# The bias of the exponentials of an attention kernel, computed on ScalarE and not on VectorE

## The chip, the cores and the metric

The kernel runs on one core of one Trainium2 chip, in one launch. The metric is the device time of the whole program in microseconds (us), the median of several runs. The engines are TensorE (matmuls; PE in the rows, with its weight loads as PEld), VectorE (DVE), ScalarE (ACT), GpSimd (POOL) and SyncE (SP), which issues DMAs. Each engine works through its own list of instructions in order and waits on semaphores for the others.

## The reference, cut to what matters

Three layers follow each other on a batch of 8 sequences of 576 positions: an attention with 8 heads of 64 and a mask by blocks of 64; four attention "experts" with a causal mask of which each position takes its best two; and a gated MLP that mixes along the sequence. The softmax is the same in both attentions:

```python
scores = scale * np.matmul(q, k.transpose(0, 1, 3, 2))
scores = np.where(mask, scores, -1000000000.0)
scores = scores - np.max(scores, axis=-1, keepdims=True)
attn = np.exp(scores)
attn = attn / (np.sum(attn, axis=-1, keepdims=True) + 1e-09)
return np.matmul(attn, v).astype(np.float32)
```

What matters here is the exponential of a score less the maximum of its row. The kernel computes exp(es * s + bias) with bias = nes * m + ln 32, where s are the raw products, m the maximum of a row, es a scale (one number, kept in each partition) and nes its negative. The factor 32 keeps the weights in the range of float16 and goes out again in the division by the sum.

## The kernel before, in words

Heads are worked on in pairs, two heads in the two halves of the partitions. Each of the 8 batches has 4 pairs of the first attention and 2 pairs of experts: 48 pairs. The matmuls take each operand as a sum of two float16 parts, so a product is three matmuls (PROD).

A pair is cut into steps. `scores(p, j)` for j = 0 to 3 takes a part of the rows each (PART: chunk 3; chunks 2 and 0; chunk 1; and the last 64 rows of both heads). It is a generator with four pieces: (1) the matmuls of the scores into one of the four PSUM buffers "duo" (L366 to L384); (2) the maxima of the rows, tensor_reduce on VectorE (L387, L389); (3) the bias for all rows of the step in one small instruction of 1, 2 or 4 elements in each partition (L396, on `st`: plane 0 holds the maxima, plane 1 the biases); (4) the exponentials on ScalarE (L399, L404), from PSUM to a buffer `pf`. With the last exponential the step gives its duo back. So there are 48 x 4 = 192 instructions L396, and 16 of the 48 pairs take es and nes from a tile `mt` instead of `es`.

After that, `weights` rounds `pf` to float16 (L329 on ScalarE, L331 on VectorE or L333 on GpSimd) and subtracts for the second part (L423, VectorE or GpSimd). `weights_t` transposes both by DMA into `pT` (L430), `av` multiplies by the values (L441) and divides (L457 to L464). Beside this run the dense steps: evictions of the transposed inputs (L229, L235), the maxima of the inputs (L283), the projections (L793, L816), and the MLP (L872, L951, L967, L987; its output is evicted by L990).

The order of all pieces is a table of numbers (ORDER): every entry runs the next piece of one step, and each engine gets its instructions in that order. A second table (WAYS) says which engine does which copy. The costs given to `add` were used to make the table; when the kernel is built they only count the pieces.

Of the kernel before, what the change touches and what calls it, by code (L numbers as in the profile page):

```python
# [8 lines left out]
F32 = mybir.dt.float32  # L9
# [7 lines left out]
AF = mybir.ActivationFunctionType  # L17
OP = mybir.AluOpType
# [3 lines left out]
P = 128  # L22
# [10 lines left out]
def attn_moe_gmlp_kernel(  # L33
# [17 lines left out]
    V, A, G, T = nc.vector, nc.scalar, nc.gpsimd, nc.tensor  # L51
# [20 lines left out]
    cst = ctx.enter_context(tc.tile_pool(name="cst", bufs=1))  # L72
# [11 lines left out]
    def mine(tag, i=0):  # L84

        return TILES[tag][:, CUR[0].got[tag][i]]
# [3 lines left out]
    def duo():  # L90
        return mine("duo")
# [252 lines left out]

    LN32 = 3.4657359027997265
    PROD = ((0, 0), (0, 1), (1, 0))

    def scores(p, j):

        ps = duo()  # L350
        ph = ps.rearrange("p (h n) -> p h n", h=2)
        if j == 0:
            p.st = sm.tile([P, 2, 9], F32, name="st")
            p.pf = {}
        pf = p.pf[j] = mine("pf")
        st = p.st
        off = {}
        o = 0
        for c in PART[j]:
            off[c] = o  # L360
            w = P * (c + 1)
            ts = slice(P * c, P * c + P)
            for i, (a, bb) in enumerate(PROD):
                for hh in range(2):
                    hs = slice(64 * hh, 64 * hh + 64)
                    T.matmul(ph[:, hh, o:o + w], p.q[hs, a, ts], p.k[hs, bb, 0:w], start=i == 0, stop=False)  # L366
            for hh in range(2):
                hs = slice(64 * hh, 64 * hh + 64)
                if p.moe:
                    T.matmul(ph[:, hh, o + w - 128:o + w - 64], t_row[hs, 0], t_col[hs], start=False, stop=False)  # L370
            for hh in range(2):
                hs = slice(64 * hh, 64 * hh + 64)
                if p.moe:
                    T.matmul(ph[:, hh, o + w - 64:o + w], t_row[hs, 1], t_col[hs], start=False, stop=True)
                else:
                    T.matmul(ph[:, hh, o + w - 64:o + w], m_row[hs], m_col[hs], start=False, stop=True)  # L376
            o += w
        if j == 3:
            for a, n in HALF:
                for i, (l, r) in enumerate(PROD):  # L380
                    T.matmul(ps[:, MID + a:MID + a + n], p.q[:, l, 512:640], p.k[:, r, a:a + n], start=i == 0,
                             stop=i == 2 and not (p.moe and a))
            if p.moe:
                T.matmul(ps[:, MID + 512:MID + S], identb, t_pk, start=False, stop=True)  # L384
        yield
        for c in PART[j]:
            V.reduce_max(st[:, 0, 2 * c:2 * c + 2], ph[:, :, off[c]:off[c] + P * (c + 1)], axis=AX.X)  # L387
        if j == 3:
            V.reduce_max(st[:, 0, 8:9], ps[:, MID:MID + S], axis=AX.X)  # L389
        yield  # L390
        if j == 1:
            m, o = (st[:, z, 0:8].rearrange("p (a c) -> p a c", a=2)[:, :, 0:2] for z in range(2))
        else:
            s = (slice(6, 8), None, slice(2, 4), slice(8, 9))[j]
            m, o = st[:, 0, s], st[:, 1, s]
        V.tensor_scalar(o, m, p.nes, LN32, op0=OP.mult, op1=OP.add)  # L396
        yield
        if j == 3:
            A.activation(pf[:, 448:1024], ps[:, MID:MID + S], AF.Exp, bias=st[:, 1, 8:9], scale=p.es)  # L399
        n = sum(P * (c + 1) for c in PART[j])  # L400
        for c in PART[j]:
            w = P * (c + 1)
            for hh in range(2):
                A.activation(pf[:, n * hh + off[c]:n * hh + off[c] + w], ph[:, hh, off[c]:off[c] + w], AF.Exp,  # L404
                             bias=st[:, 1, 2 * c + hh:2 * c + hh + 1], scale=p.es)
# [4 lines left out]
    def weights(p, j, way):  # L410

        if j == 0:
            p.p16 = {}
        g = GROUP[j]
        if j < 3:
            p.p16[g] = mine("p16")
        s0, n, o0, per = WCOL[j]
        src = p.pf[j][:, s0:s0 + n]
        t = p.p16[g]
        hi, lo = t[:, o0:o0 + n], t[:, per + o0:per + o0 + n]  # L420
        copy16(hi, src, way[0])
        yield
        (V if way[1] == "D" else G).tensor_sub(lo, src, hi)  # L423

    def weights_t(p, g):
        if g == 0:
            p.pT = {}
        t = p.pT[g] = mine("pT")
        n = 16 if g < 2 else 18
        nc.sync.dma_start_transpose(out=t[:, 0:n * P].rearrange("p (n s) -> p n s", s=P), in_=p.p16[g][:, 0:n * P])  # L430
# [49 lines left out]
    def startup():  # L480
# [227 lines left out]
        def s_wm(n):  # L708
# [3 lines left out]
            for c in range(KH):  # L712
                i = 0
                for d in range(KD):
                    for x, y in PROD:
                        T.matmul(ps[:, c], t["woT"][:, x, d, c, :], hl[:, y, d, :], start=i == 0, stop=i == 11)
# [37 lines left out]
    def dense(b, keep):  # L754
# [25 lines left out]
        def proj(n, i):  # L780
# [8 lines left out]
            for a, w in HALF:  # L789
                m = 0  # L790
                for c in range(KD):
                    for l, r in PROD:
                        T.matmul(ps[:, MID + a:MID + a + w], wqk16[:, l, c, 2 * n + i, :], x16[c][:, r, a:a + w],  # L793
# [15 lines left out]
        def vproj(cs):  # L809
            n = len(cs)  # L810
            ps = duo().rearrange("p (c m) -> p c m", c=2)[:, 0:n]
            for i, c in enumerate(cs):
                m = 0
                for d in range(KD):
                    for l, r in PROD:
                        T.matmul(ps[:, i, :260], x16[d][:, l, P * c:P * c + P], wvg16[:, r, d, :], start=m == 0,  # L816
# [45 lines left out]
        def hv(cs):  # L862
# [5 lines left out]
            for i, c in enumerate(cs):  # L868
                m = 0
                for d in range(KH):  # L870
                    for l, r in PROD:
                        T.matmul(ps[:, i], h16[d][:, l, P * c:P * c + P], wf16[:, r, d, FH:], start=m == 0, stop=m == 5)  # L872
# [357 lines left out]
    def pe(*cols, more=0.0):  # L1230
        return ("PE", more + sum(max(n / 2400 + 0.002, 0.029) for n in cols))

    def act(n, ops=1, each=0.13):
        return ("ACT", 0.000833 * n + each * ops)

    def dve(n=8, ops=1, rate=1.04):
        return ("DVE", (rate * n + 80 * ops) / 1000)
# [62 lines left out]
    def copy_sub(n, hi="ADG", more=()):  # L1300

        a = dict(A=act(n), D=dve(n, rate=0.62), G=pool(n, rate=1.1))
        b = dict(D=dve(n, rate=1.35), G=pool(n))
        return {x + y: [a[x], b[y]] + list(more) for x in hi for y in "DG"}


    def pair_steps(key, due, sc_deps, av_deps, wt, moe):

        def p():
            return PD[key]  # L1310
        for j in range(4):
            n = (1024, 1024, 512, 576)[j]
            cols = ((512,) * 3, (384, 128) * 3, (256,) * 3, (288, 288) * 3)[j] + (64,) * (0 if j == 3 and not moe else (1 + (j == 1)) * (1 + moe))
            ops = (1, 2, 1, 1)[j]
            add(("sc", key, j), due + 3 * j, lambda j=j: scores(p(), j),
                [pe(*cols, more=0.2 * (j < 3)), dve(n, ops), dve(), act(n, (2, 4, 2, 1)[j], 0.21)],
                sc_deps, [("sc", key, j - 1)] if j else [], ["duo", "pf"] + [("st", key)] * (j == 0), ["duo"])
        add(("fr", "st", key), due, None, deps=[("sc", key, j) for j in range(4)], rel=[("st", key)])
        add(("fr", "qk", key), due, None, deps=[("sc", key, j) for j in range(4)], rel=[("qk", key)])
        for j in range(4):  # L1320
            n = (1024, 1024, 512, 640)[j]
            add(("w", key, j), due + 3 * j + 4, lambda w, j=j: weights(p(), j, w), copy_sub(n),
                [("sc", key, j), ("su", "abm", 0), ("su", "abm", 1)], [("w", key, 2)] if j == 3 else [], [("p16", (key, j))] if j < 3 else [],
                [("pf", ("sc", key, j))], way=("AG", "DG", "AG", "DD")[j])
        for g in range(3):
            add(("wt", key, g), due + 4 * g + 7, lambda g=g: weights_t(p(), g), [spt((16, 16, 18)[g])],
                [("w", key, j) for j in range(4) if GROUP[j] == g] + [("su", "pad")], [], [("pT", (key, g))], [("p16", (key, g))])
        n = 65
        add(("av", key), due + 18, lambda: av(p(), wt),
            [pe(*[65] * 24), pe(*[65] * 24), pe(*[65] * 42)] + [dve()] * (2 + (wt is not None)) + [dve(640)],  # L1330
            [("wt", key, g) for g in range(3)] + av_deps, [], ["duo", ("x32", key)],
            ["duo"] + [("pT:%d" % g, (key, g)) for g in range(3)])
        add(("x", key), due + 22, lambda w: halves(p(), w), copy_sub(640, more=[spt(10)]),
            [("av", key), ("su", "split", 0), ("su", "split", 1)], [],
            [("xh", key), ("x", key)], [("x32:1", key), ("xh", key)], way="GG")
# [206 lines left out]
```

## Time and profile before

| | us |
|---|---|
| median of 3 runs | 1118.19 |
| lowest and highest | 1117.58 and 1120.28 |
| the profiled execution | 1121.58 |
| its span, first to last instruction | 1119.9 |
| mean granted TensorE clock in it | 0.908 |

The profile is of one execution. Busy times of the engines are sums over their instructions; a stretch is a part of the span; the chain is followed back from the last instruction, at each step to what released it. A wait is the idle time of an engine just before an instruction, put down to the instruction that ended it.

### The profile page before, as it was taken

What the parts mean: (1) busy time and instruction counts of PE and PEld (TensorE: products, weight loads), DVE (VectorE), ACT (ScalarE), POOL (GpSimd) and SP (SyncE); (2) the same over time, 40 slices, a digit from 0 to 9 for tenths busy, and PEclk for the clock granted to TensorE, in tenths of its full rate; (3) what the DMA queues carried; (4) which work ended last, traced back from release to release, by engine and by line L of the source; (5) the groups of instructions that cost most, each with busy time, mean ns of one, the idle gap of its engine ahead of it and who ended that gap; (6) DMA issues with size and microseconds to landing.
All of it is one profiled execution on the core that took longest, in us unless ns stands there. A gap on an engine that the chain in (4) does not pass through costs nothing.

```text
span 1119.9 us, 25239 instructions
## 1 busy us (share of the span) xinstructions
PE 906.4 (81%) x10122; PEld 654.0 (58%) x10122; DVE 885.8 (79%) x1776; ACT 591.0 (53%) x999; POOL 481.7 (43%) x373
## 2 busy tenths in 40 slices
PE   1555568867989888887898887889897999899778
PEld 1344446655666666555675665656774677666444
DVE  2799899899999889888978797968887788657451
ACT  3576566454655555554646455546655564344222
POOL 3636555364254426452544325442775353423110
PEclk9688676878999989998999998999898989999979
DMA  9557969797568948589458974986666456802701
GB/s 197 133 134 146 183 156 154 133 176 158 87 138 161 184 85 144 95 177 166 99 117 157 174 130 93 143 172 116 131 135 142 96 91 116 168 17 39 147 1 43
DMA packets 503028, 143.64 MB, mean 128 GB/s; under 512 B 491200, under 2 KB 497392, under 8 KB 502912
## 3 DMA queue, kind: packets, MB, share of 16 engines
q1 hardware_dynamic: 486176, 134.62, 63.4%
q10 hardware_dynamic: 15296, 3.65, 2.0%
q0 software_dynamic: 1440, 3.78, 1.2%
q8 instruction: 79, 1.29, 0.5%
q14 instruction: 37, 0.30, 0.1%
HBM read 38.19 MB, written 9.44 MB: 43 GB/s over the span
## 4 chain that ended last, share of the span: by engine, by line
PE 25%; DVE 21%; ACT 6%; DMA 5%; issue 4%; POOL 3%; SPq 2%; ACTq 0%; DVEq 0%; POOLq 0%
PE duo L967 5%; PE duo L987 4%; DVE st L387 4%; PE duo L441 3%; PE duo L872 3%; ACT pf L404 3%; DMA pT<-p 3%; PE duo L793 2%; DVE p L331 2%; PE duo L366 2%; DVE p L423 2%; PE duo L816 2%; PE duo L951 1%; DVE st L396 1%; DVE vn L916 1%
## 5 line engine op out<-in xcount | busy, mean ns | idle before, releaser
L423 POOL TENSOR_TENSOR p<-pf,p 128x1024 f16<-128x1024 f32 (+2 forms) x121 | 228.4, 1892 | 210.8 <-ACT p L329 93.8
L404 ACT ACTIVATE pf<-duo,st,es 128x128 f32<-128x128 f32 (+3 forms) x256 | 139.0, 620 | 106.6 <-DVE st L396 77.3
L441 PEld LDWEIGHTS <-pT 128*128 128x128 f16 x4320 | 153.1, 101 | 38.5 <-DMA pT<-p 16.8
L387 DVE TENSOR_REDUCE st<-duo 128x2 f32<-128x1024 f32 (+1 forms) x192 | 151.0, 815 | 14.8 <-PE duo L376 7.5
L967 PE MATMUL duo<-wsp,vn 128*128 128x288 f16 x896 | 127.9, 299 | 18.0 <-DVE x L464 6.5
L366 PE MATMUL duo<-qk 64*128 64x256 f16 (+3 forms) x1152 | 112.3, 312 | 36.3 <-DVE qk L806 11.9
L987 PE MATMUL duo<-wo,gT 128*128 128x512 f16 (+1 forms) x480 | 114.1, 395 | 8.9 <-ACT pf L404 7.3
L793 PE MATMUL duo<-x,wqk 128*128 128x288 f16 x768 | 106.3, 302 | 16.6 <-ACT pf L399 13.9
L441 PE MATMUL duo<-v,pT 128*128 128x65 f16 (+1 forms) x2880 | 108.3, 199 | 13.7 <-DMA pT<-p 7.5
L967 PEld LDWEIGHTS <-vn 128*128 128x128 f16 x896 | 90.1, 102 | 46.4 <-issue 12.8
L404 ACT ACTIVATE pf<-duo,st,mt 128x512 f32<-128x512 f32 (+3 forms) x128 | 69.8, 619 | 72.0 <-DVE st L396 58.6
L793 PEld LDWEIGHTS <-wqk 128*128 128x128 f16 x768 | 78.4, 103 | 42.0 <-issue 18.2
L333 POOL TENSOR_SCALAR p<-pf 128x1024 f16<-128x1024 f32 (+2 forms) x41 | 43.9, 1071 | 126.0 <-ACT pf L404 76.1
L423 DVE TENSOR_TENSOR p<-pf,p 128x640 f16<-128x640 f32 (+2 forms) x71 | 83.5, 1178 | 10.2 <-ACT p L329 4.9
L987 PEld LDWEIGHTS <-gT 128*128 128x128 f16 (+1 forms) x480 | 48.5, 104 | 66.0 <-issue 15.7
L331 DVE CAST p<-pf 128x512 f16<-128x512 f32 (+2 forms) x82 | 64.5, 791 | 28.1 <-ACT pf L404 12.8
L366 PEld LDWEIGHTS <-qk 64*128 64x128 f16 x1152 | 47.8, 97 | 66.1 <-issue 51.4
L283 DVE TENSOR_REDUCE mst<-nat 128x1 f32<-128x640 f32 (+1 forms) x56 | 61.2, 1095 | 26.8 <-DMA nat<-in_k_dram 16.5
L910 POOL TENSOR_SCALAR vf<-vf,nw 128x512 f32<-128x512 f32 (+1 forms) x35 | 33.3, 958 | 80.5 <-DVE nw L901 62.5
L322 PE MATMUL duo<-ident,nat 128*128 128x128 f32 (+1 forms) x320 | 53.2, 302 | 14.6 <-ACT pf L404 5.4
L441 PE MATMUL duo<-V,pT 128*128 128x65 f16 (+1 forms) x1440 | 53.9, 198 | 12.8 <-DMA pT<-p 8.0
L816 PE MATMUL duo<-wvg,x 128*128 128x260 f16 x480 | 60.9, 287 | 3.7 <-ACT pf L404 2.6
(250 smaller groups left out, 1737.4 us busy)
## 6 DMA issues: line engine op xcount, KB each, us to landing
out_dram<-o SPq DMA_DIRECT2D x16, 512.0 KB, 3.9
nat<-in_q_dram SPq DMA_DIRECT2D x58, 128.0 KB, 3.3
nat<-in_k_dram SPq DMA_DIRECT2D x58, 128.0 KB, 3.2
nat<-in_v_dram SPq DMA_DIRECT2D x50, 128.0 KB, 3.0
wf<-in_moe_w_in_dram SPq DMA_DIRECT2D x8, 512.0 KB, 5.8
pT<-p SPq DMA_TRANSPOSE x144, 4.8
wf<-in_moe_w_out_dram SPq DMA_DIRECT2D x4, 512.0 KB, 4.4
pT<-in_moe_w_spatial_dram POOLq DMA_DIRECT2D x1, 1152.0 KB, 7.5
```

The costliest lines, as they stand in the source:

```text
L283: V.tensor_reduce(s.st[:, a, pr:pr + 1], t[:, a].rearrange("p i c d -> p i (c d)"), op=OP.max, axis=AX.X, apply_absolute_value=True)
L322: T.transpose(ps[:, P * c:P * c + r], p.nat[0:r, i, c, :], ident[0:r, 0:r])
L331: V.tensor_copy(hi, src)
L366: T.matmul(ph[:, hh, o:o + w], p.q[hs, a, ts], p.k[hs, bb, 0:w], start=i == 0, stop=False)
L387: V.reduce_max(st[:, 0, 2 * c:2 * c + 2], ph[:, :, off[c]:off[c] + P * (c + 1)], axis=AX.X)
L404: A.activation(pf[:, n * hh + off[c]:n * hh + off[c] + w], ph[:, hh, off[c]:off[c] + w], AF.Exp, bias=st[:, 1, 2 * c + hh:2 * c + hh + 1], ...
L423: (V if way[1] == "D" else G).tensor_sub(lo, src, hi)
L441: T.matmul(ps[:, hh, o:o + n], pT[:, col(t, kk):col(t, kk) + P], p.v[:, hh, kk, a:a + n], start=kk == 0 and i == 0, stop=kk == nk - 1 and ...
L793: T.matmul(ps[:, MID + a:MID + a + w], wqk16[:, l, c, 2 * n + i, :], x16[c][:, r, a:a + w], start=m == 0, stop=m == 11)
L816: T.matmul(ps[:, i, :260], x16[d][:, l, P * c:P * c + P], wvg16[:, r, d, :], start=m == 0, stop=m == 11)
L967: T.matmul(ps[:, MID + a:MID + a + n], vn[:, l, ds_], wsp16[:, r, c, a:a + n], start=i == 0, stop=False)
L987: T.matmul(ps[0:r, i], gT[:, x, d, P * c:P * c + r], wo16[:, y, d, :], start=m == 0, stop=m == 11)
```

## The change

A tile of one column, `ln32`, is filled with ln 32 once. The small instruction of piece (3) is no longer a tensor_scalar of VectorE (times nes, plus a constant) but an activation of ScalarE with the function Identity, scale nes and bias `ln32`. The table of the order and the ways stay as they are. In the call of `add` the third piece has ScalarE's cost in place of VectorE's.

```diff
     LN32 = 3.4657359027997265
     PROD = ((0, 0), (0, 1), (1, 0))
+    ln32 = cst.tile([P, 1], F32, name="ln32")
+    V.memset(ln32, LN32)
...
-        V.tensor_scalar(o, m, p.nes, LN32, op0=OP.mult, op1=OP.add)
+        A.activation(o, m, AF.Identity, bias=ln32, scale=p.nes)
         yield
...
-                [pe(*cols, more=0.2 * (j < 3)), dve(n, ops), dve(), act(n, (2, 4, 2, 1)[j], 0.21)],
+                [pe(*cols, more=0.2 * (j < 3)), dve(n, ops), act(8), act(n, (2, 4, 2, 1)[j], 0.21)],
```

The lines of the kernel move down by two, so that L396 becomes L398, L399 and L404 become L401 and L406, and L423 becomes L425.

The first place is the one at 620 to 628 us of the trace. On VectorE before, L396 stands three times, each a few instructions behind its reduction; the third (128x1) belongs to the reduction L389 and stands behind a cast:

```order
L396 TENSOR_SCALAR st<-st,es 128x2x2
L387 TENSOR_REDUCE st<-duo 128x2
L235 SCALAR_TENSOR_TENSOR v<-nat,scb,v 128x10x64
L396 TENSOR_SCALAR st<-st,es 128x2
L283 TENSOR_REDUCE mst<-nat 128x1
L389 TENSOR_REDUCE st<-duo 128x1
L331 CAST p_140<-pf 128x512
L396 TENSOR_SCALAR st<-st,es 128x1
L423 TENSOR_TENSOR p_140<-pf,p_140 128x512
```

And VectorE at the same place now:

```order
L389 TENSOR_REDUCE st<-duo 128x2
L235 SCALAR_TENSOR_TENSOR v<-nat,scb,v 128x10x64
L283 TENSOR_REDUCE mst<-nat 128x1
L391 TENSOR_REDUCE st<-duo 128x1
L331 CAST p_140<-pf 128x512
L425 TENSOR_TENSOR p_140<-pf,p_140 128x512
```

The three are gone and the others keep their order. On ScalarE at that place before (the maxima are those of the rows above, `o` is the output of the MLP):

```order
L404 ACTIVATE pf<-duo,st,es 128x384 x2
L404 ACTIVATE pf<-duo,st,es 128x128 x2
L404 ACTIVATE pf<-duo,st,es 128x256 x2
L990 ACTIVATE o<-duo,hs 128x1024
L399 ACTIVATE pf<-duo,st,es 128x576
```

ScalarE now:

```order
L398 ACTIVATE st<-st,ln_182,es 128x2x2
L406 ACTIVATE pf<-duo,st,es 128x384 x2
L406 ACTIVATE pf<-duo,st,es 128x128 x2
L398 ACTIVATE st<-st,ln_182,es 128x2
L406 ACTIVATE pf<-duo,st,es 128x256 x2
L992 ACTIVATE o<-duo,hs 128x1024
L398 ACTIVATE st<-st,ln_182,es 128x1
L401 ACTIVATE pf<-duo,st,es 128x576
```

Each bias stands right in front of the exponentials that use it. The second place is at 476 us, on ScalarE, where an expert's first bias and the evictions of transposed inputs (`qk`, for the next pair) are near each other. Before:

```order
L990 ACTIVATE o<-duo,hs 128x1024
L229 ACTIVATE qk<-duo,scb 128x640
L229 ACTIVATE qk<-duo,scb 128x576
L404 ACTIVATE pf<-duo,st,mt 128x512 x2
L229 ACTIVATE qk<-duo,scb 128x640
```

Now:

```order
L992 ACTIVATE o<-duo,hs 128x1024
L398 ACTIVATE st<-st,ln_182,mt 128x2
L229 ACTIVATE qk<-duo,scb 128x640
L229 ACTIVATE qk<-duo,scb 128x576
L406 ACTIVATE pf<-duo,st,mt 128x512 x2
L229 ACTIVATE qk<-duo,scb 128x640
```

Here the bias stands in front of two evictions that do not need it.

## Rows read from the trace of the kernel before

**Rows 1.** The page: busy us of each engine (share of the span), instructions

```profile
PE 906.4 (81%) x10122; PEld 654.0 (58%) x10122; DVE 885.8 (79%) x1776; ACT 591.0 (53%) x999; POOL 481.7 (43%) x373
```

**Rows 2.** Stretches: start:end, length, busy us of PE, PEld, DVE, ACT, POOL; clock; DMA

```profile
70.00:400.00 330.00, 248.59 (x2988) 188.24 (x2987) 301.24 (x553) 191.58 (x330) 156.86 (x109) 0.84 0.79 152
400.00:1060.00 660.00, 582.83 (x6734) 418.78 (x6732) 523.26 (x1071) 351.49 (x597) 289.74 (x210) 0.95 0.66 123
```

**Rows 3.** The page: the chain that ended last, by engine and by line

```profile
PE 25%; DVE 21%; ACT 6%; DMA 5%; issue 4%; POOL 3%; SPq 2%; ACTq 0%; DVEq 0%; POOLq 0%
PE duo L967 5%; PE duo L987 4%; DVE st L387 4%; PE duo L441 3%; PE duo L872 3%; ACT pf L404 3%; DMA pT<-p 3%; PE duo L793 2%; DVE p L331 2%; PE duo L366 2%; DVE p L423 2%; PE duo L816 2%; PE duo L951 1%; DVE st L396 1%; DVE vn L916 1%
```

**Rows 4.** Waits: who for whom, us in total, times, longest

```profile
ACT pf L404 <- DVE st L396: 135.9, 66, 5.7
ACT pf L399 <- DVE st L396: 51.4, 23, 6.8
...
PE duo L793 <- ACT pf L399: 13.9, 5, 4.9
...
PE duo L381 <- ACT pf L404: 0.4, 1, 0.4
```

**Rows 5.** Groups of VectorE, L396: busy us, mean ns | idle before

```profile
L396 DVE TENSOR_SCALAR st<-st,es 128x2 f32<-128x2 f32 (+2 forms) x128 | 44.3, 357 | 0.5
L396 DVE TENSOR_SCALAR st<-st,mt 128x2 f32<-128x2 f32 (+1 forms) x64 | 26.6, 421 | 0.5
```

**Rows 6.** Line L396, its larger half: shortest, median, longest in ns

```profile
L396 DVE TENSOR_SCALAR st<-st,es x128: 166/220/2102, 68.4 to 946.2; 128x2 f32<-128x2 f32 x64, 128x4 f32<-128x4 f32 x32, 128x1 f32<-128x1 f32 x32
```

**Rows 7.** Timeline of VectorE and ScalarE, 622 to 628: start, us, engine, line

```profile
622.44 0.75 DVE L389 TENSOR_REDUCE st<-duo 128x1 f32<-128x576 f32 x1
626.79 0.43 DVE L331 CAST p<-pf 128x512 f16<-128x512 f32 x1 [3.61 <-DMA pT<-p]
627.13 0.21 DVE L396 TENSOR_SCALAR st<-st,es 128x1 f32<-128x1 f32 x1
627.26 0.69 DVE L423 TENSOR_TENSOR p<-pf,p 128x512 f16<-128x512 f32 x1
...
623.10 1.14 ACT L990 ACTIVATE o<-duo,hs 128x1024 f32<-128x1024 f32 x1
627.46 0.83 ACT L399 ACTIVATE pf<-duo,st,es 128x576 f32<-128x576 f32 x1 [3.23 <-DVE st L396]
```

**Rows 8.** Timeline of VectorE and GpSimd at 488 us

```profile
488.08 2.13 POOL L423 TENSOR_TENSOR p<-pf,p 128x1024 f16<-128x1024 f32 x1
488.48 1.76 DVE L396 TENSOR_SCALAR st<-st,mt 128x2 f32<-128x2 f32 x1
490.15 0.74 DVE L389 TENSOR_REDUCE st<-duo 128x1 f32<-128x576 f32 x1
```

**Rows 9.** Groups of ScalarE by shape: exponentials of 512 and 128 columns

```profile
L404 ACT ACTIVATE pf<-duo,st,es 128x512 f32<-128x512 f32 x64 | 46.4, 777 | 47.7 <-DVE st L396 27.2 <-DVE hm L927 6.6 <-DVE rr L459 5.6
L404 ACT ACTIVATE pf<-duo,st,es 128x128 f32<-128x128 f32 x64 | 25.9, 464 | 0.0
```

**Rows 10.** Timeline of ScalarE: two exponentials in a row

```profile
68.74 1.45 ACT L404 ACTIVATE pf<-duo,st,es 128x512 f32<-128x512 f32 x2 [1.31 <-DVE st L396]
```

**Rows 11.** Pieces of the chain that ended last: start, us, what

```profile
383.86 0.23 DVE st L396
...
1042.83 0.23 DVE st L396
```

**Rows 12.** The stretch 70 to 400, instructions of L396 alone

```profile
70.00:400.00 330.00, 28.69 (x71) 0.84 0.79 152
```

**Rows 13.** Timeline of VectorE and ScalarE at 476 us

```profile
476.59 1.21 DVE L387 TENSOR_REDUCE st<-duo 128x2 f32<-128x1024 f32 x1
...
477.20 1.43 ACT L229 ACTIVATE qk<-duo,scb 128x640 f16<-128x640 f32 x2 [1.84 <-PE duo L322]
```

**Rows 14.** Groups of ScalarE: the table load

```profile
L586 ACT ACT_TABLE_LOAD x1 | 1.3, 1283 | 18.8 <-DMA nat<-in_v_dram 18.8
```

## The prediction

> **What bounds the kernel now.** I read the busy shares first. TensorE is busy 81% of the span and VectorE 79%, ScalarE only 53% and GpSimd 43% [rows 1]. An average hides two stages, so the stretches come next [rows 2]. From 70 to 400 us VectorE is busy 301.2 of 330 us (91%) and TensorE 248.6 (75%): VectorE is the bound there. From 400 to 1060 us TensorE has 582.8 of 660 (88%), VectorE 523.3 (79%): TensorE leads, and what it waits for counts. The last 60 us are dense work without an exponential. Third is the chain that ended last [rows 3]: TensorE 25% and VectorE 21% of the span, ScalarE 6%. Its shares add up to 66% and its first piece is at 378 us, so it says nothing of the first third. On it the bias (L396) has 1% under its own name. Last the waits [rows 4]: ScalarE sat idle in front of exponentials until a bias of VectorE for 135.9 + 51.4 = 187.3 us, in 89 waits. TensorE in turn waits for exponentials to give a PSUM buffer free: 13 rows, 39 waits, 58.3 us, the first and last of them shown.
>
> The reader is to see a loop: scores, reduction, bias, exponential, buffer free, next matmul. ScalarE is the one engine in it with room.
>
> **What is removed.** 192 small instructions leave VectorE, 44.3 + 26.6 = 70.9 us busy [rows 5]. That is 0.37 us each while the median is 0.220 and the longest 2.1 [rows 6]: a few are long because they stand still. Short ones hold the engine less than they last: at 627.13 one lasts 0.21 and the next instruction starts at 627.26, 0.13 later [rows 7]. So about 192 x 0.13 = 25 us is the pitch, and 70.9 - 192 x 0.21 = 31 us is standing still, 56 us together. One of the long ones shows the cause: it starts at 488.48 and lasts 1.76, ending at 490.24; a subtraction of GpSimd runs from 488.08 to 490.21, and the reduction queued behind starts at 490.15 [rows 8].
>
> The Trainium skill (SBUF — State Buffer, "Who interferes with whom") says that VectorE and GpSimd share one pair of ports as a lock, that a tensor_scalar in a two-port mode may take it and a tensor_reduce never does; by that rule a stall in front of a reduction vanishes with the bias and one in front of a cast may only move to the cast. The ends at 490.24 and 490.21 agree with the lock; that it moves no run here shows yet.
>
> **What is added.** 192 activations on ScalarE, of 1 to 4 elements, with a bias and a scale from memory. The trace has no such size; the exponentials have the same two operands. They last 777 ns at 512 columns and 464 at 128 [rows 9], 0.815 ns a column, so 464 - 126 x 0.815 = 361 ns at 2 columns. Two that follow each other take 1.45 us where 2 x 0.777 were 1.55 [rows 10]: 0.10 overlap, a pitch of 0.26. The dependent exponential may overlap too or not: 0.26 to 0.40; I take 0.31. On ScalarE this is 192 x 0.36 = 69 us more busy time, 591 to 660, 59% of the span. The overlap of 0.10 is seen between instructions without such a dependence, which is why I stay in the middle.
>
> **What moves.** TensorE, GpSimd and the DMA queues keep their instructions and order; no DMA is moved past anything. The one new constant is a memset of VectorE at the start. What changes is where the bias waits. Before, it queued on VectorE behind whatever lay between the reduction and it. At 622.44 a reduction starts and ends at 623.19. Behind it a cast waits for a buffer until 626.79, the bias comes at 627.13, and the exponential at 627.46, although ScalarE had been free since 624.24 [rows 7]. Now the bias stands on ScalarE behind the output eviction: 624.24 + 0.31 = 624.6, 2.9 us earlier. Only a part is worth anything, since that cast still ends at 627.22 and VectorE goes on from there. The opposite case is at 383.86: there the bias was the very next thing after its reduction, 0.23 on the chain [rows 11], and 0.36 replaces it: 0.1 lost. The added wait is that ScalarE now stops at the bias for the reduction. Mostly the exponential is next and would have waited anyway; in 32 of 192 places, by the new order, something else is next.
>
> **The sum.** (a) 70 to 400 us: 71 of the biases, 28.7 us busy [rows 12]. Pitch 71 x 0.13 = 9, stalls 28.7 - 71 x 0.21 = 14: 23 us of a VectorE that is 91% busy. The ends are 0 (the stalls move on and other engines fill the rest) and 23; I take half, 11, since 9% of idle time already shows other limits.
> (b) From 378 us the chain has 49 pieces of L396, 15.1 us in all, the first at 383.86, the last at 1042.83 [rows 11]. 30 of them hand on to VectorE itself, 6.3 us, and simply go. 19 hand on to an exponential, 8.8 us; each becomes 0.31, so 5.9 comes back and 2.9 is the least gain. Where other VectorE work stood between reduction and bias, as at 627, more goes: up to 15 if every such exponential moved its whole way. I take 7. Against it, where ScalarE itself is on the chain without waiting for a bias, a dozen new activations at 0.26 add 3. That is 6.3 + 7 - 3 = 10, of which some is lost when another chain ends last: 8, between -3 and 18.
> (c) From 1060 us: nothing.
> Together 19 us. The profiled execution took 1121.6 us (span 1119.9 and 1.7 around it), 3.4 above the median of the runs, 1118.2; so 1121.6 - 19 = 1102.6 in its terms, and 1099 for the median.
>
> **The rivals.**
> *The stall moves on.* Of (a) only the pitch is left, 9, half of it 5, and (b) loses the long pieces, as the 1.76 at 488.48: about 4. Sum 9: 1109. For it: half the chain goes on with VectorE work, casts among it. Against it: at 488 and 623 the next instruction or the waiting exponential does not need GpSimd. [...]
> *It is hidden anyway.* TensorE has 88% from 400 us on, and the exponentials come earlier into a VectorE queue whose order was laid out for the later time; at 627 the work behind is held by a transpose DMA. Then the gain is under 0.3% (3.4 us, about what a measurement can tell): 1117. Against it: 58.3 us of TensorE's waits are for exponentials.
> *ScalarE's queue stops: slower.* In the 32 places a bias now stands in front of work that was free to run. At 476.59 a reduction starts and ends at 477.80; two evictions of transposes went at 477.20 [rows 13]. With the bias ahead of them they start at 477.80 + 0.36, 1.0 us later, and with them their PSUM buffer. If 20 of the 32 cost 1 us on the path, (a) and (b) are eaten up; if all do, 32 - 19 = 13 slower, and with the 103 biases (192 - 89) whose exponential did not wait a part of 103 x 0.26 = 27 comes on top. I price it at +8: 1126. Against it: ScalarE is busy only 53%.
> The skill's ScalarE: Activation LUTs ("Rules for kernel authors") sends add and multiply to VectorE, not ScalarE, which speaks against this change. By the rows it is 0.36 against 0.21 each; if length alone decided, 49 pieces on the chain would make 49 x 0.15 = 7 us, 1125, which shares this rival's chance. At 627 it is not length that decides but the queue in front of the bias.
> *It does not do what it says:* exponentials with another function between them could reload ScalarE's table. The one load of the trace takes 1.28 us [rows 14]; 192 pairs would give 490 us. The kernel already mixes exponentials, Relu and absolute values with that one load, and the new order has one too. No chance given.
>
> **How the numbers follow.** Forecast (1099, its own range 1090 to 1108) 0.52; the stall moves on (1109) 0.25; hidden (1117) 0.13; slower (1126) 0.10. The first two are faster by over 0.3%: 0.77. Same: 0.13, slower: 0.10. The range takes (a) and (b) near their upper ends, 1118 - 36 = 1082, with under 0.1 left below, and reaches into the hidden case, 1119; what is left above is the slower one.
>
> **What would show it.** L396 gone from VectorE, its busy time down by some 60 to 70 us, its idle time up by less. ScalarE up by 60 to 70 us, the new activations near 0.36 us, still one table load. ScalarE's waits in front of exponentials, 187 us, now in front of the bias and for the reduction, and well under that. TensorE's 58 us of waits for exponentials shorter. Stretches: most gain from 70 to 400 us. If VectorE's casts and subtractions grow by some 20 us together, the stall moved. If evictions (L229 before) wait behind biases and TensorE's waits for them grow, the slower rival is right. The forecast is wrong if VectorE's time falls as said and the span does not.

## The result, and the profile after

The changed kernel takes 1107.63 us (median of 4 runs, 1105.66 to 1110.61), beside 1119.24 for the kernel before on the same chip: 0.9900 of its time [0.9872, 0.9927], some 11 us faster where 19 were forecast. The profiled execution took 1110.61 us (span 1108.9). Like the one of before it is about 3 us above its median, so the two compare evenly.

Busy us of each engine after, to hold against [rows 1]:

```profile
PE 898.7 (81%) x10122; PEld 647.5 (58%) x10122; DVE 846.5 (76%) x1585; ACT 656.4 (59%) x1191; POOL 483.1 (44%) x373
```

VectorE has 191 instructions fewer (192 less the memset) and 39.3 us less busy time, ScalarE 192 more and 65.4 us more. The two stretches after, in the columns of [rows 2]:

```profile
70.00:400.00 330.00, 246.28 (x3024) 184.77 (x3024) 288.22 (x488) 218.61 (x408) 158.84 (x109) 0.88 0.79 152
400.00:1060.00 660.00, 584.67 (x6742) 418.18 (x6741) 502.66 (x958) 393.46 (x715) 289.23 (x210) 0.95 0.67 123
```

In the first, VectorE fell from 301.2 to 288.2, 13 us, and is still busy 87%. The new instruction after (shortest, median, longest in ns; compare [rows 6]):

```profile
L398 ACT ACTIVATE st<-st,ln,es x128: 370/388/407, 69.5 to 944.2; 128x2 f32<-128x2 f32 x64, 128x4 f32<-128x4 f32 x32, 128x1 f32<-128x1 f32 x32
```

It lasts 0.388 us and never stands still. And the waits after (compare [rows 4]): ScalarE's in front of the bias, then the first and the last row of TensorE's for exponentials:

```profile
ACT st L398 <- DVE st L389: 104.2, 71, 5.9
ACT st L398 <- DVE st L391: 50.7, 24, 7.1
...
PE duo L795 <- ACT pf L401: 13.4, 3, 5.4
...
PE duo L953 <- ACT pf L406: 0.8, 1, 0.8
```

ScalarE waits 154.9 us in 95 waits where it was 187.3 in 89. TensorE waits for exponentials in 14 rows, 37 waits, 59.5 us together, against 58.3 before. One of the 37 is the same wait under another name. Before:

```profile
240.46 0.37 PE L197 MATMUL duo<-ident,m 128*3 128x128 f32 x1 [6.74 <-DVE m L290]
```

And after:

```profile
238.96 0.37 PE L197 MATMUL duo<-ident,m 128*3 128x128 f32 x1 [9.61 <-ACT pf L406]
```

TensorE stood idle in front of this matmul in both, before put down to VectorE and after to an exponential. Without it, TensorE's waits for exponentials are 49.9 us, 8 less than before. Kernels that gained nothing or little have sums below 58.3 too (e1, further down, 55.1; e8 52.0), so one profile each does not show whether the gain came through that door.

Where VectorE's room went shows in its groups: busy us, mean ns, then idle us in front of the group and what ended it. Before:

```profile
L423 DVE TENSOR_TENSOR p<-pf,p 128x640 f16<-128x640 f32 (+2 forms) x71 | 83.5, 1178 | 10.2 <-ACT p L329 4.9 <-POOL p L333 4.4 <-issue 0.4
L331 DVE CAST p<-pf 128x512 f16<-128x512 f32 (+2 forms) x82 | 64.5, 791 | 28.1 <-ACT pf L404 12.8 <-DMA pT<-p 5.7 <-ACT pf L399 4.4
L283 DVE TENSOR_REDUCE mst<-nat 128x1 f32<-128x640 f32 (+1 forms) x56 | 61.2, 1095 | 26.8 <-DMA nat<-in_k_dram 16.5 <-DMA nat<-in_v_dram 7.3 <-DMA nat<-in_q_dram 2.2
...
L916 DVE TENSOR_TENSOR vn<-vf,vn 64x512 f16<-64x512 f32 x7 | 15.6, 2229 | 6.1 <-ACT vn L913 6.0
```

And after:

```profile
L425 DVE TENSOR_TENSOR p<-pf,p 128x640 f16<-128x640 f32 (+2 forms) x71 | 77.5, 1093 | 8.4 <-ACT p L329 5.0 <-POOL p L333 2.7
L331 DVE CAST p<-pf 128x512 f16<-128x512 f32 (+2 forms) x82 | 65.8, 807 | 36.8 <-ACT pf L406 12.9 <-ACT pf L401 9.4 <-DMA pT<-p 5.9
L283 DVE TENSOR_REDUCE mst<-nat 128x1 f32<-128x640 f32 (+1 forms) x56 | 61.3, 1097 | 35.3 <-DMA nat<-in_k_dram 21.1 <-DMA nat<-in_v_dram 10.0 <-DMA nat<-in_q_dram 4.0
...
L918 DVE TENSOR_TENSOR vn<-vf,vn 64x512 f16<-64x512 f32 x7 | 20.2, 2893 | 6.5 <-ACT vn L915 6.4
```

VectorE stands 8.5 us more in front of the input maxima, waiting for loads, and 8.7 more in front of the casts. The casts and the subtractions of weights did not grow (148.0 to 143.3 us together). Seven subtractions of 64 partitions in the MLP's normalization (`vn`, L916, now L918) did, from 15.6 to 20.2.

Next, how the lead of after over before runs along TensorE: the same instruction in both timelines (start, us, what). Before:

```profile
398.23 5.36 PE L816 MATMUL duo<-wvg,x 128*128 128x260 f16 x24 [1.67 <-ACT pf L404]
...
785.76 6.05 PE L793 MATMUL duo<-x,wqk 128*128 128x288 f16 x48
...
796.95 1.52 PE L366 MATMUL duo<-qk 64*128 64x512 f16 x5 [2.95 <-DVE qk L806]
...
1061.86 5.31 PE L872 MATMUL duo<-wf,x 128*128 128x512 f16 x16 [2.89 <-DMA x<-xh]
```

After:

```profile
395.30 2.83 PE L818 MATMUL duo<-wvg,x 128*128 128x260 f16 x24 [1.81 <-ACT pf L406]
...
780.44 6.05 PE L795 MATMUL duo<-x,wqk 128*128 128x288 f16 x48
...
796.95 1.53 PE L368 MATMUL duo<-qk 64*128 64x512 f16 x5 [8.25 <-DVE qk L808]
...
1052.63 6.00 PE L874 MATMUL duo<-wf,x 128*128 128x512 f16 x27 [2.02 <-DMA x<-xh]
```

The lead is 2.9 us at 398, 5.3 at 786, nothing at 797, 9.2 at 1062 and 11.0 at the end. Between 786 and 797 all of it is gone: TensorE waits 8.25 us for one VectorE instruction, where before it waited 2.95. VectorE and GpSimd at that place, after:

```profile
787.93 8.18 DVE L918 TENSOR_TENSOR vn<-vf,vn 64x512 f16<-64x512 f32 x1 [1.34 <-ACT vn L915]
796.14 2.09 DVE L808 SCALAR_TENSOR_TENSOR qk<-duo,mt,qk 128x512 f16<-128x512 f32 x4
...
787.95 1.15 POOL L918 TENSOR_TENSOR vn<-vf,vn 128x512 f16<-128x512 f32 x1
789.06 1.14 POOL L425 TENSOR_TENSOR p<-pf,p 128x512 f16<-128x512 f32 x1
790.16 1.55 POOL L266 DMA_DIRECT2D nat<-in_v_dram  x2
791.70 0.61 POOL L269 DMA_DIRECT2D nat<-in_v_dram  x1
792.32 1.16 POOL L918 TENSOR_TENSOR vn<-vf,vn 128x512 f16<-128x512 f32 x1
793.43 2.12 POOL L425 TENSOR_TENSOR p<-pf,p 128x1024 f16<-128x1024 f32 x1
```

The same instruction before:

```profile
793.59 2.53 DVE L916 TENSOR_TENSOR vn<-vf,vn 64x512 f16<-64x512 f32 x1 [0.89 <-ACT vn L913]
...
793.31 1.15 POOL L916 TENSOR_TENSOR vn<-vf,vn 128x512 f16<-128x512 f32 x1
794.42 1.15 POOL L423 TENSOR_TENSOR p<-pf,p 128x512 f16<-128x512 f32 x1
795.52 1.56 POOL L266 DMA_DIRECT2D nat<-in_v_dram  x2
```

The shortest of its line takes 0.68 us. Before, it stood until GpSimd turned to issuing DMAs, and ended at 796.12. After, it arrived 5.7 us earlier, did not get in when GpSimd turned to the same DMAs at 790.16, stood through two more subtractions, and ended at 796.11. What all the rest had gained by then was waited away there. The seven have a second long one, at 677 us before (4.80 us) and at 671 after (4.81); it is in both, so it does not part them.

### The profile page after: what moved, and what is told of

Read it like the earlier page. It is cut to its first block, busy times and chain, and to the rows that moved or that the text cites. A ratio compares the mean times of both kernels' runs of the same rounds, so it can differ in the third digit from the quotient of the medians.

```text
span 1108.9 us, 25219 instructions
## 1 busy us (share of the span) xinstructions
PE 898.7 (81%) x10122; PEld 647.5 (58%) x10122; DVE 846.5 (76%) x1585; ACT 656.4 (59%) x1191; POOL 483.1 (44%) x373
## 5 line engine op out<-in xcount | busy, mean ns | idle before, releaser
L425 POOL TENSOR_TENSOR p<-pf,p 128x1024 f16<-128x1024 f32 (+2 forms) x121 | 229.8, 1904 | 209.2 <-ACT p L329 81.3
L443 PEld LDWEIGHTS <-pT 128*128 128x128 f16 x4320 | 151.5, 101 | 39.2 <-DMA pT<-p 17.1
L389 DVE TENSOR_REDUCE st<-duo 128x2 f32<-128x1024 f32 (+1 forms) x192 | 150.3, 814 | 19.4 <-PE duo L378 9.3
L406 ACT ACTIVATE pf<-duo,st,es 128x128 f32<-128x128 f32 (+3 forms) x256 | 139.5, 616 | 3.6 <-ACT st L398 0.4
L443 PE MATMUL duo<-v,pT 128*128 128x65 f16 (+1 forms) x2880 | 107.5, 198 | 16.8 <-DMA pT<-p 8.8
L398 ACT ACTIVATE st<-st,ln,es 128x2 f32<-128x2 f32 (+2 forms) x128 | 48.3, 387 | 95.8 <-DVE st L389 57.1
L331 DVE CAST p<-pf 128x512 f16<-128x512 f32 (+2 forms) x82 | 65.8, 807 | 36.8 <-ACT pf L406 12.9
L425 DVE TENSOR_TENSOR p<-pf,p 128x640 f16<-128x640 f32 (+2 forms) x71 | 77.5, 1093 | 8.4 <-ACT p L329 5.0
L406 ACT ACTIVATE pf<-duo,st,mt 128x512 f32<-128x512 f32 (+3 forms) x128 | 70.2, 616 | 7.9 <-issue 6.3
L476 POOL TENSOR_TENSOR xh<-x,xh 128x640 f16<-128x640 f32 x30 | 45.8, 1528 | 40.6 <-DVE xh L331 37.2
```

Source lines behind the costliest of these rows:

```text
L331: V.tensor_copy(hi, src)
L398: A.activation(o, m, AF.Identity, bias=ln32, scale=p.nes)
L443: T.matmul(ps[:, hh, o:o + n], pT[:, col(t, kk):col(t, kk) + P], p.v[:, hh, kk, a:a + n], start=kk == 0 and i == 0, stop=kk == nk - 1 and ...
```

## The experiments

Two theories stood at first. A, the load: the gain is VectorE's time, pitch and standing still. B, the place: the gain is that the bias no longer queues behind VectorE's other work. After the first four runs came S, the stall: the one subtraction above takes back part of whatever is gained, so kernels must be compared with it out of the way. "Before" and "changed" are the two kernels of the case; each ratio is against before on the same chip. Differences between ratios carry both intervals, added as squares.

**e1_both.** The changed kernel, with the old instruction left on VectorE, its output read by nobody.

```diff
+        V.tensor_scalar(u, m, p.nes, LN32, op0=OP.mult, op1=OP.add)
         A.activation(o, m, AF.Identity, bias=ln32, scale=p.nes)
```

> The bias on ScalarE as in the changed kernel, and the old instruction also left on VectorE at its old place, writing to a plane that nothing reads. Theory A (the gain is VectorE's room: pitch and standing still of 192 instructions): the gain goes, ratio to the kernel before 0.997 to 1.002. Theory B (the gain is that the bias no longer queues on VectorE behind other work, so exponentials start earlier): the gain stays, 0.988 to 0.993. In between, both in their shares.

Measured: 1.0047 [1.0023, 1.0071], 1122.8 us. All of the gain is gone and a little more (above theory A's range), although the bias stands where the change puts it. So the place alone is not the gain; putting VectorE's instruction back costs 0.0147 ± 0.0037.

**e2_dve_next.** Before, with the bias still on VectorE but directly behind its reduction.

```diff
             V.reduce_max(st[:, 0, 8:9], ps[:, MID:MID + S], axis=AX.X)
-        yield
         if j == 1:
...
         yield
+        yield
         if j == 3:
```

> The bias stays on VectorE, but is issued in the same piece as its reduction, right behind it, so that nothing queues in between. Theory A: VectorE holds the same 192 instructions, no gain, 0.997 to 1.002. Theory B: most of the gain without ScalarE, 0.988 to 0.993.

Measured: 1.0115 [1.0086, 1.0143], 1128.58 us: the earliest place for the bias is the slowest kernel of all, outside the ranges of both theories. Its groups:

```profile
L395 DVE TENSOR_SCALAR st<-st,es 128x2 f32<-128x2 f32 (+2 forms) x128 | 52.7, 411 | 4.5
L395 DVE TENSOR_SCALAR st<-st,mt 128x2 f32<-128x2 f32 x64 | 28.6, 447 | 2.3
```

One place of its timeline:

```profile
76.18 0.75 DVE L389 TENSOR_REDUCE st<-duo 128x1 f32<-128x576 f32 x1
76.96 0.21 DVE L395 TENSOR_SCALAR st<-st,es 128x1 f32<-128x1 f32 x1
```

The bias now takes 81.3 us (70.9 before), and behind its own reduction it starts 0.03 us after that ended, while elsewhere neighbours overlap by 0.08 or 0.09 [rows 7]. VectorE's busy time rose by 21.2 us to 907.0. This speaks for the load and against the place. That it explains the whole 0.0115 is not shown; this profile has the long stall too (8.59 us).

**e3_act_last.** Changed, with the bias moved into the last piece, so that no other ScalarE work stands between it and its exponentials (the slower rival's 32 places are gone).

```diff
-        A.activation(o, m, AF.Identity, bias=ln32, scale=p.nes)
         yield
+        A.activation(o, m, AF.Identity, bias=ln32, scale=p.nes)
         if j == 3:
```

> The changed kernel with the bias issued in the last piece, right in front of its exponentials, so that in none of the 32 places other work of ScalarE stands behind a bias that waits. If those stops cost (the slower rival of the prediction, in part): 0.984 to 0.988. If they cost nothing: as the changed kernel, 0.989 to 0.991. Theories A and B do not differ here.

Measured: 0.9859 [0.9833, 0.9884], 1101.12 us, 0.0041 ± 0.0038 better than changed. But in its profile the subtraction near 788 us takes 2.41 us and not 8.18, so this is not yet the queue's price; e7 asks again.

**e5_act_twice.** Changed, with the bias computed twice on ScalarE.

```diff
+        A.activation(u, m, AF.Identity, bias=ln32, scale=p.nes)
         A.activation(o, m, AF.Identity, bias=ln32, scale=p.nes)
```

> The changed kernel with every bias computed twice on ScalarE, the first into a plane that nothing reads: 192 more activations, some 55 us more of ScalarE's time and 0.29 us later exponentials. If ScalarE has room (both theories as I stated them): 0.990 to 0.994. If the length of the bias on ScalarE counts on the path, 49 pieces of 0.29: 14 us, 1.002.

Measured: 0.9960 [0.9937, 0.9983], 1112.01 us. 192 more activations cost 0.0060 ± 0.0036, and here too the long stall is absent (1.18 us). With the stall only in one of the two, the difference is not a clean price; f4 gives that.

**e6_vn_gpsimd.** Changed, with the 64-partition subtractions always on GpSimd (the second letter of each pair; seven instructions change engine).

```diff
-        "norm.4": ("GG", "DD", "GD", "GD"), ...
+        "norm.4": ("GG", "DG", "GG", "GG"), ...
```

> The changed kernel with one more edit: the last subtraction of the normalised gate (vn, 64 rows, once in each batch) always on GpSimd. In the profile of the changed kernel one of these stood still for 8.2 us on VectorE at 788 us and the lead over the kernel before, 5.3 us, was gone behind it; it did so too with the bias on both engines (8.2) and behind its reduction (8.6), and not with the bias in the last piece or twice. Theory S (that one stall hides half of the change's gain): 0.983 to 0.987, as the version with the bias in the last piece. Theory Q (that version was better because ScalarE's queue no longer stops at a bias): 0.989 to 0.992, as the changed kernel.

Measured: 0.9841 [0.9801, 0.9880], 1100.21 us, 0.0059 ± 0.0048 better than changed. The line in changed and in this kernel:

```profile
L918 DVE TENSOR_TENSOR vn<-vf,vn x11: 676/1220/8184, 309.2 to 1069.7; 64x512 f16<-64x512 f32 x7, 128x512 f16<-128x512 f32 x4
```

```profile
L918 DVE TENSOR_TENSOR vn<-vf,vn x4: 693/1056/1635, 306.6 to 1060.6; 128x512 f16<-128x512 f32 x4
```

And TensorE's waits for `qk` in this kernel:

```profile
PE duo L368 <- DVE qk L808: 7.5, 6, 2.2
```

TensorE's longest wait for `qk` of VectorE is 2.2 us; in changed it was 8.3, as in e1, e2, e8 and e9; before it was 2.9. VectorE is busy 833.6 us, 12.9 less than in changed.

**e7_last_vn_gpsimd.** e3 with the edit of e6.

```diff
-        A.activation(o, m, AF.Identity, bias=ln32, scale=p.nes)
         yield
+        A.activation(o, m, AF.Identity, bias=ln32, scale=p.nes)
...
+        "norm.4": ("GG", "DG", "GG", "GG"), ...
```

> The bias in the last piece, right in front of its exponentials, and vn on GpSimd as in the run before this one. Theory S: no better than vn on GpSimd alone, 0.983 to 0.987. Theory Q: both gains add or the vn edit does nothing, 0.980 to 0.986 and at least 0.004 below vn on GpSimd alone.

Measured: 0.9815 [0.9779, 0.9851], 1096.74 us: the fastest kernel of the study. That is below theory S's range, but not the 0.004 below e6 that theory Q asked for: against e6 it is 0.0026 ± 0.0053 better, which is unclear. So the queue stops of the slower rival cost between nothing and some 9 us; that they cost anything is not shown.

**e8_odd_form.** Before, with the bias on VectorE in a form that does not stand still: the maxima read three times over, 6 or 12 elements, into a tile of its own.

```diff
+                src = m.unsqueeze(1).to_broadcast([P, 3, 2])
+            V.tensor_scalar(ob[:, 0:6 * k].rearrange("p (x y) -> p x y", x=3) if j != 1 else
...
-        V.tensor_scalar(o, m, p.nes, LN32, op0=OP.mult, op1=OP.add)
```

> The kernel before, the bias still on VectorE at its old place, but read three times over (6 or 12 elements out, a source of three rows) into a tile of its own, so that the instruction does not stand still for GpSimd, as its one-element form never did. Theory L (the standing still, 31 of 56 us, is what the change saves): 0.992 to 0.996. Theory P (the pitch of 192 instructions counts as well, or alone): 0.997 to 1.001. If these instructions still last over 0.3 us, the form did not do its work and the run tells nothing.

Measured: 0.9971 [0.9948, 0.9994], 1115.8 us. The form does what it should:

```profile
L404 DVE TENSOR_SCALAR ob<-st,es x96: 158/213/226, 71.4 to 941.4; 128x6 f32<-128x6 f32 x64, 128x12 f32<-128x12 f32 x32
```

Longest 226 ns where it was 2102 [rows 6]. VectorE's busy time fell by 17.1 us, the time by 3 (with the 8.2 us stall in this profile too). The 192 instructions themselves fell from 70.9 to 40.2 us, so the 31 us of standing still that I had counted did go. The engine got 17 of them back; the rest came up again in other instructions, 6.7 us of it in the `vn` subtractions (19.1 to 25.9 us).

**e9_both_odd.** e1, with VectorE's extra instruction in the form of e8.

```diff
+            V.tensor_scalar(ob[:, 0:6 * k].rearrange("p (x y) -> p x y", x=3) if j != 1 else
...
+            V.tensor_scalar(u, m, p.nes, LN32, op0=OP.mult, op1=OP.add)
         A.activation(o, m, AF.Identity, bias=ln32, scale=p.nes)
```

> The bias on ScalarE and the old instruction left on VectorE as well, but in the form of the run before, which does not stand still; its result is read by nothing. Theory L: most of the gain stays, 0.990 to 0.996 (the run with the form that stands still gave 1.0047). Theory P: the gain goes, 0.999 to 1.005.

Measured: 0.9995 [0.9969, 1.0022], 1118.22 us, 0.0052 ± 0.0036 better than e1: the standing still. The rest to changed, 0.0095 ± 0.0038, is the pitch, if the stall (8.20 us here too) weighs the same in both.

**f1 to f4.** Before, e1, e9 and e5, each with the edit of e6, so that the stall is in none of them. The diff is the same in all four.

```diff
-        "norm.4": ("GG", "DD", "GD", "GD"), ...
+        "norm.4": ("GG", "DG", "GG", "GG"), ...
```

> The kernel before with vn on GpSimd, as control: all four runs of this call have that edit, so that the one long stall at 788 us can't be in some and not in others. With the bias on ScalarE this edit gave 0.9841. Theory S (the edit only takes away a stall that the kernel before hardly had): 0.995 to 1.000. If the edit is good by itself: 0.990.

Measured: 0.9993 [0.9970, 1.0017], 1117.47 us: without the change the edit is worth nothing.

> The bias on both engines, the old form on VectorE, vn on GpSimd. The difference to 0.9841 is the price of the 192 instructions on VectorE, pitch and standing still. Theory A: 0.996 to 1.001, so 12 to 17 thousandths. Theory B (their room is worth nothing): 0.984.

Measured: 0.9956 [0.9931, 0.9980], 1114.5 us, 0.0037 ± 0.0034 better than f1: the bias on ScalarE alone, barely clear. It is just outside theory A's range.

> The same with the form on VectorE that does not stand still: the difference to 0.9841 is the price of the pitch alone, some 25 us of VectorE, and the difference to the run before is the price of standing still, some 31 us. Theory L (standing still is what counts): 0.986 to 0.990. Theory P (pitch counts at least as much): 0.992 to 0.996.

Measured: 0.9922 [0.9895, 0.9949], 1110.65 us, 0.0034 ± 0.0036 better than f2: the standing still, not clear by itself. It is in theory P's range.

> The bias twice on ScalarE, vn on GpSimd: the difference to 0.9841 is the price of 192 more activations on ScalarE, some 52 us of its time, with no stall in the way. If ScalarE has room: 0.984 to 0.988. If the length counts on the path, 49 pieces of 0.29: 0.995 to 0.998.

Measured: 0.9948 [0.9924, 0.9972], 1111.48 us, 0.0107 ± 0.0046 slower than e6: 192 more activations. So ScalarE did not have room, and the time is close to the range for a length that counts on the path. In it a bias stands twice in a row. The second of the two activations, right behind the first (L398):

```profile
L399 ACT ACTIVATE st<-st,ln,es 128x2 f32<-128x2 f32 (+2 forms) x128 | 48.4, 378 | 0.0
```

What the edit of the subtractions is worth, by whether the kernel's profile without it shows the long stall at that place:

| kernel | that subtraction in its profile, us | its start, less that of GpSimd's `vn` subtraction beside it, us | gain of the edit |
|---|---|---|---|
| before | 2.53 | +0.28 | 0.0007 ± 0.0024 |
| e5 | 1.18 | +0.51 | 0.0012 ± 0.0033 |
| changed | 8.18 | -0.02 | 0.0059 ± 0.0048 |
| e9 | 8.20 | -0.03 | 0.0073 ± 0.0038 |
| e1 | 8.25 | -0.08 | 0.0091 ± 0.0034 |
| e3 | 2.41 | +0.39 | 0.0044 ± 0.0044 |

Five of the six fit S: 7 to 10 us where it takes 8 us, nothing clear where it is not. e3 lies between. Each profile is one execution, and whether the other executions of a kernel have the stall is not seen. The third column goes with the second without exception, e2 (-0.43, 8.59 us) and e8 (-0.04, 8.20 us) included: where VectorE's subtraction starts ahead of GpSimd's it stands for over 8 us, where it starts behind it is let in after 1.2 to 2.5. No run moved it on purpose, so this is a pattern of eight profiles and not yet a cause.

With the stall out of the way the change comes apart (1 in 1000 is 1.1 us):

| step | from, to | ratio | us |
|---|---|---|---|
| the whole change | f1, e6 | -0.0152 ± 0.0046 | 17 |
| bias read from ScalarE, VectorE's instruction stays | f1, f2 | -0.0037 ± 0.0034 | 4 |
| VectorE's instruction stops standing still | f2, f3 | -0.0034 ± 0.0036 | 4 |
| VectorE's instruction goes altogether | f3, e6 | -0.0081 ± 0.0048 | 9 |
| 192 more activations on ScalarE | e6, f4 | +0.0107 ± 0.0046 | 12 |

e6 ran in another group and on another chip than the f kernels, each against its own runs of before. A holds: 13 of the 17 us are VectorE's load (f2 to e6, 0.0115 ± 0.0046). B has a share that is just clear of zero. VectorE's busy time in the same steps, one profile each: f2 877.1, f3 860.3, e6 833.6 us, so 16.8 for the standing still and 26.7 for the pitch, 0.139 us each. A few us of such differences come by themselves: f1 has 884.5 and f2 877.1, with the same work on VectorE but for one memset.

## Why the prediction was right in sign and 8 us off in size

**The sign and what bounds.** Taking instructions away from VectorE is most of the gain: e1 and f2 show it. It did not come where VectorE is the bound in [rows 2]: "most gain from 70 to 400 us" failed, 4.1 of 11 us came there. The Trainium skill's rule that sends add and multiply to VectorE (ScalarE: Activation LUTs, "Rules for kernel authors") speaks against the change. It measured 0.9900 here, on a kernel whose VectorE was busy 79% and its ScalarE 53%.

**What is removed.** The pitch was right: 0.13 forecast, 0.139 from f3 to e6. The standing still was 31 us on paper; the instructions lost it, but VectorE got back only 17 of it in e8 and in f2 to f3. (The longest bias took 2.7 us, not 2.1: [rows 6] is only the larger half.) "Busy time down by some 60 to 70" did not even follow from the 56 us counted, and failed: 39.3, or 50.9 in e6 against f1 (884.5 to 833.6).

**What is added.** This term was mis-sized. I took a bias as 0.361 us and 0.31 up to its exponential, trusting half of an overlap. ScalarE after:

```profile
69.50 0.39 ACT L398 ACTIVATE st<-st,ln,es 128x2 f32<-128x2 f32 x1 [0.39 <-DVE st L389]
69.93 1.45 ACT L406 ACTIVATE pf<-duo,st,es 128x512 f32<-128x512 f32 x2
```

From bias to exponential it is 0.43, here and in the median: 0.39 and a gap, no overlap, outside my 0.26 to 0.40. And ScalarE's room was not free. I charged 3 us for a dozen biases on the chain; 192 more of them cost 12 us by f4. Part of that is that the second one stands in front of the real bias and delays it, so it is an upper mark for the change itself rather than its price.

**What moves.** At 627 it went as said, and shows how little an earlier exponential is worth. VectorE at that place before, beside [rows 7]:

```profile
628.32 0.49 DVE L331 CAST p<-pf 128x640 f16<-128x640 f32 x1 [0.38 <-ACT pf L399]
```

VectorE and ScalarE there after:

```profile
617.92 0.75 DVE L391 TENSOR_REDUCE st<-duo 128x1 f32<-128x576 f32 x1
621.51 0.43 DVE L331 CAST p<-pf 128x512 f16<-128x512 f32 x1 [2.84 <-DMA pT<-p]
...
622.58 0.49 DVE L331 CAST p<-pf 128x640 f16<-128x640 f32 x1
...
618.71 0.39 ACT L398 ACTIVATE st<-st,ln,es 128x1 f32<-128x1 f32 x1 [0.79 <-DVE st L391]
619.17 0.83 ACT L401 ACTIVATE pf<-duo,st,es 128x576 f32<-128x576 f32 x1
```

The exponential starts 0.50 us after its reduction ends instead of 4.27. The cast that reads it follows the held cast by 1.07 instead of 1.53 (before at 628.32 and 626.79): 0.46 gained of 3.77, because that held cast still waits for a transpose.

**The sum, by stretches.** (a) forecast 11, got 4.1: after was 1.2 us late at 69 (the first exponential at 69.93 for 68.74 [rows 10]) and 2.9 ahead at 398. VectorE's 13 us less became a lead only in part; its waits for loads and exponentials grew beside it (8.5 and 8.7 over the whole run). Some of the lead may even be the clock, 0.84 before and 0.88 after in this stretch; f1, which has not the change, has 0.87. (b) forecast 8, got 6.3, as +2.4, -5.3 and +9.2 around the stall. (c) forecast nothing, got 1.8 (11.0 - 9.2). The +2.4 and the 1.8 come from TensorE's clock in these two executions. The 24 matmuls at 398 us take 5.36 us before, at a granted clock of 0.50 (1.2 GHz), and 2.83 after, at 1.00 (2.4 GHz); TensorE had been idle for 1.67 and 1.81 us just before. The first sixteen at 1062 take 5.31 us before, at 0.67 on average, and 3.4 after, at 1.00. In e6, the faster kernel, the clock was low at both places (0.50 and 0.77), so the change alone does not raise it:

```profile
393.95 5.36 PE L818 MATMUL duo<-wvg,x 128*128 128x260 f16 x24 [1.82 <-ACT pf L406]
...
1040.51 7.69 PE L874 MATMUL duo<-wf,x 128*128 128x512 f16 x27 [3.49 <-DMA x<-xh]
```

These are single executions, a few us apart from run to run. ScalarE's waits, forecast "well under" 187 us, fell to 155.

**The rivals.** "The stall moves on" had the time (1109), and half of the mechanism. Of the 56 us counted, VectorE got 39.3 back. Part of the rest shows as longer instructions in many places (`vn` 4.6 us, the evictions of L235 4.0, L509 2.8), but not in casts and subtractions of weights, which I had named as the sign. What cost time was one of them, a subtraction of the MLP in a long run of GpSimd work that I never looked at. That is the failed step: I asked what stands behind each bias, not where a VectorE that runs 5 us earlier meets GpSimd next. Without it the change is worth 17 us, near the forecast 19. That nearness is partly luck: the added cost and the standing still were both mis-sized, and the stretches came out otherwise. In e6 (a) gave 6.1 us where 11 were forecast (1.8 late at 69 us, 4.3 ahead at 398), and (b) 17.1 where 8 were (21.4 ahead at 1062). "Hidden anyway" is not borne out by a gain of 11 us, and TensorE's waits for exponentials can't settle it, as said above. "ScalarE's queue stops" cost no more than the gap of e6 and e7. Its places are more than the 32 counted: in the trace of the changed kernel 57 biases are followed by something other than an exponential, 27 of them by another bias.

**Open.** Why a start ahead of GpSimd's goes with a stall that outlasts even the DMA issues at 790.16, when before the subtraction got in at 795.52; how much of e2's loss its 8.59 us are. And how much of the 17 us goes through TensorE's clock: over all runs the granted clock averaged 0.9207 in e6 and 0.9105 in the runs of before beside it, and no run here separates its share.

## What to carry to other kernels

Price an instruction on a loaded engine by its pitch and its standing still, and check it against the stretch: here 43.5 us of VectorE's time (f2 to e6) were worth 13, and 52 us on a ScalarE that is busy 60% cost up to 12. A small instruction in front of the one that reads its result costs its full length and a gap, 0.43 us here, not the pitch of independent ones. When a change lets an engine run earlier, follow both timelines instruction by instruction and look for the place where the lead vanishes; moving seven subtractions to GpSimd gave 0.0059 ± 0.0048 on top of the change's 0.0100, and nothing without the change. e7 (bias in the last piece, subtractions on GpSimd) measured lowest, 0.9815, but can't be told from e6, 0.9841.

## What the runs showed of the hardware that was not expected

A subtraction of 64x512 with two inputs in SBUF stood on VectorE for 8.18 us, through four GpSimd subtractions and the DMA issues between them; five of the profiled kernels have it, at 8.18 to 8.59. The Trainium skill (SBUF — State Buffer, "Who interferes with whom") says that a VectorE instruction with two SBUF inputs contends with a GpSimd one that reads SBUF, and that the first to issue shuts the other out for its whole length. Its end at 796.11, 0.56 us behind that of the last GpSimd subtraction (795.55), agrees. In the five profiles it had started 0.02 to 0.43 us before the first of the GpSimd subtractions that it stood through, and lost to it all the same (a tensor_scalar of GpSimd was still running at its start in each); so the order of issue alone does not give the winner here. That one instruction can lose turn after turn, and the DMA issues between, is what the rows add.

The bias on VectorE in 2 or 4 elements lasted up to 2.7 us. The half of its line that [rows 6] does not show, before:

```profile
L396 DVE TENSOR_SCALAR st<-st,mt x64: 155/220/2681, 208.9 to 1042.8; 128x2 f32<-128x2 f32 x32, 128x4 f32<-128x4 f32 x16, 128x1 f32<-128x1 f32 x16
```

In 6 or 12 elements with an outermost dimension of 3 in the source it never took over 0.226. The Trainium skill (VectorE: DVE Perf Modes, "What auto-detection actually checks") lets one source and a destination in SBUF take the two-port mode when their outermost dimensions are both even or equal. If the destination of e8, which is contiguous, counts as one dimension of 6 or 12 against the source's 3, they are neither, and the numbers agree; how it is counted is not in the trace.
